# Gated attention and spectral mixing on one core: key differences, the half-scanned pair and output weights handled at other places in the program

## The chip, the core and the metric

The kernel runs on one core of a Trainium2 chip. The metric is the device time of one execution in microseconds (us). A core has five engines with instruction streams of their own: TensorE (PE, with its weight loads as PEld), VectorE (DVE), ScalarE (ACT), GpSimd (POOL) and SyncE (SP), which here only issues DMAs. Each stream runs in order, and an instruction that waits holds up everything behind it in that stream.

## The reference, cut to what matters

```python
x = A_x                                              # (1, 2048, 512)
g = sigmoid((x * gate_w).sum(-1, keepdims=True))
qkv = x @ wqkv                                       # 32 heads of 16
a = softmax(q @ k.T / 4) @ v                         # full attention per head
a = a.reshape(1, 2048, 512) @ wo
b = cr @ (x @ wr.T) - ci @ (x @ wi.T)                # real part of a 2-D Fourier transform
out = g * a + (1 - g) * b                            # cr, ci: 2048 x 2048
```

The weights of the projections are scaled by 64, so scores are large and the softmax needs the maximum of every row.

## The kernel before, in words

All products are done in fp32r with each operand split into a rounded part (hi) and a rest (lo); hi·hi, hi·lo and lo·hi are added. A product of one 128x512 tile therefore takes 12 steps of two matmuls each (`products`, `halves_of` at L180; the two matmuls of a step use the upper and the lower half of the array). One such step is called a **slot** here, and 12 slots a **unit**. `beside()` is called after each slot. It counts slots, runs whatever `after(n, f)` has put off by n slots, and puts in a **scan** when the pace says so. A scan is a score tile of one head pair (two matmuls, 48 rows each) of which DVE takes the row maxima; there are 64 scans a pair and 16 pairs. `scan_at(3.9)` asks for one scan every 3.9 slots.

The program has these stages in order.

1. **Projections** (0 to about 303 us): first q and k (`project_t`), then v (t = 0 to 15), then x·wr and x·wi (`project_s`, 16 units each). ACT copies a unit's two half sums out of PSUM (tags xy, two buffers), POOL adds them, ACT and POOL split them and SP stores them to DRAM. Scans 0 to about 184 run beside these units.
2. **Spectral products** (to about 711 us): 96 units of `coef` for the first 24 of 32 half tiles. The scans 192 to 691 are **folded**: the keys of two key blocks are replaced by one block and a difference of keys (kf_d), ACT takes a relu of the difference scores and DVE adds and reduces in one instruction (L153, L155). In the middle the operands in SBUF are swapped for the second half (`renew`).
3. **Attention** (to the end): 512 steps, 32 a head pair. A step has the scores of one key block (L637), three ACT exponentials (L641, L645), the product with the values (L652) and, up to step 331, one more plain scan (L130). From step MIX = 333 on the other spectral products and, from OUT = 461 on, the output projection (`mix_heads`) are put between.

Three things matter for the change.

- **Differences of keys.** In `project_t` for k the sum s of an odd block c is followed by `fold_keys` (L346): POOL subtracts the two sums that are kept in `half`, ACT makes hi (L215 eh), POOL or DVE makes lo (fl), SP stores both (L356). There are eight folds, two beside the first four k units and six beside the last twelve; during these twelve the pace is SLOW_PACE = 5.2.
- **The half-scanned pair.** FRONT = 692 scans are done when stage 2 ends, so pair 10 is scanned to 52 of 64 with folded keys and needs plain keys for the last 12. `load_scan(10)` (L860, loads at L95 in SP's queue) does that after the loop, into buffers of tag stk (six buffers, two a pair). `load_scan_beside(11)` has loaded pair 11 on ACT's queue shortly before, and step 2 of the attention loads pair 11 once more.
- **Output weights and sums.** `output_operands` is a generator of which one part runs at each step from OUT - 12 on: load a block of wo (tag craw, two buffers), cast it on DVE in the next step (L697, L713), subtract in the one after (L699, L715). `output_rows` loads rows of the attention output (L724), `load_y` (L737) loads two blocks of 1 MB of spectral sums at OUT - 3.

SP's queue holds almost all DMA issues, and so an issue that waits for a buffer holds up all later ones.

Of the kernel before, what the change touches and what calls it, by code (L numbers as in the profile page):

```python
# [18 lines left out]
P = 128  # L19
S = 2048  # L20
# [18 lines left out]
FOLD_PACE = 2.18  # L39
SLOW_PACE = 5.2  # L40
# [7 lines left out]
def build(tc, x, xT, wqkv, wo, wrT, wiT, cr, ci, gate, out):  # L48
    nc = tc.nc
    with ExitStack() as ctx:  # L50
# [7 lines left out]
        k_d = [dram.tile([P, 2, S], F32, name=f"k_d{f}") for f in range(ND)]  # L58
        kf_d = [dram.tile([P, 2, S], F32, name=f"kf_d{f}") for f in range(ND)]
# [22 lines left out]
        scanned, used = {}, {}  # L82
# [107 lines left out]
        with ExitStack() as pf:  # L190
# [34 lines left out]
            def beside():  # L225
# [89 lines left out]
            with ExitStack() as px:  # L315
# [30 lines left out]
                half = {}  # L346

                def fold_keys(f, c):

                    a, b = half.pop(c - 1), half.pop(c)  # L350
                    hi = ep.tile([P, 512], F32R, tag="eh", name="eh", bufs=3)
                    lo = ep.tile([P, 512], F32R, tag="ty", name="fl")
                    nc.gpsimd.tensor_sub(a, a, b)

                    def store(i, v):
                        nc.sync.dma_start(kf_d[f][:, i, (c - 1) * 512:c * 512], v.bitcast(F32))  # L356

                    after(7, nc.scalar.copy, hi, a)
                    after(12, (nc.vector if f else nc.gpsimd).tensor_sub, lo, a, hi.bitcast(F32))
                    after(13, store, 0, hi)  # L360
                    after(16, store, 1, lo)

                def project_t(w, dst, f, c, ps=None):
# [5 lines left out]
                    s = rp.tile([P, 512], F32, tag="raw", name="s") if folded else ep.tile([P, 512], F32, tag="ty", name="s")  # L369
# [92 lines left out]
                scan_at(PACE)  # L462
# [16 lines left out]
                for t in range(NB):  # L479
                    load_xn(t)  # L480
                    after(30, gate_sum, t)
# [44 lines left out]
            with ExitStack() as py:  # L526
# [22 lines left out]
                for n, (ph, t, u) in enumerate(coef):  # L549
# [6 lines left out]
                    if n == len(coef) - 2 * NU:  # L556
                        load_use(0)
# [14 lines left out]
                    def renew(s):  # L572
                        split_operand(s, early.pop(s), nc.gpsimd if s % 4 == 3 else nc.vector)
# [26 lines left out]
        with ExitStack() as pa:  # L600
# [88 lines left out]

            def output_operands():  # L690

                for f in range(ND - 1):
                    raw = ap.tile([P, D], F32, tag="craw", name="wor", bufs=2)
                    nc.sync.dma_start(raw, wo[f * P:f * P + P, :].rearrange("(h e) m -> e h m", e=DH))
                    yield
                    w = [block(6 + 2 * f + i) for i in range(2)]
                    nc.vector.tensor_copy(w[0], raw)  # L697
                    yield
                    nc.vector.tensor_sub(w[1], raw, w[0].bitcast(F32))  # L699
                    w2.append(w)  # L700
                for n in range(3):
                    raw = ap.tile([P, D], F32, tag="craw", name="wor", bufs=2)
                    base = D - (8, 4, 2)[n] * DH
                    if n:
                        nc.vector.memset(raw, 0.0)
                        for c, j, r in quads:
                            nc.sync.dma_start(raw[r:r + DH, :], wo[base + DH * j:base + DH * j + DH, :])
                    else:
                        for r in (0, 64):
                            nc.sync.dma_start(raw[r:r + 64, :], wo[base:base + 64, :].rearrange("(h e) m -> e h m", e=DH))  # L710
                    yield
                    w = [block(12 + 2 * n + i) for i in range(2)]
                    nc.vector.tensor_copy(w[0], raw)  # L713
                    yield
                    nc.vector.tensor_sub(w[1], raw, w[0].bitcast(F32))  # L715
                    w4.append(w)
# [142 lines left out]
            if FRONT % SCANS:  # L859
                load_scan(FRONT // SCANS)  # L860
# [21 lines left out]
            for step in range(NP * PERIODS):  # L882
# [115 lines left out]
```

## Time and profile before

| | |
|---|---|
| median of three runs | 1801.66 us (1800.71 to 1802.69) |
| the profiled execution, its own time | 1800.78 us |
| its span in the trace | 1799.0 us |
| PE busy | 1731.1 us, 96% |
| ACT, DVE, POOL busy | 1453.3, 1165.8, 708.6 us |
| mean granted clock of PE | 0.985 |

The profile is of one execution. Busy time of PE is from the modelled ends of matmuls, so that a PE which is "busy" may still wait a little; the number of matmuls in a stretch of given length tells more. "Idle before" names what ended an idle time. A row of the timeline gives the start in us, the length, the engine, the line and what was done. The granted clock is 1.00 at full speed and 0.50 where PE was held to half.

### The profile page before, as it was taken

To read this page: it belongs to the slowest core of one execution; us is meant where nothing else is said; L and a number is where in the kernel's file an instruction comes from. 1 tells how busy PE (TensorE), PEld (TensorE's weight loads), DVE (VectorE), ACT (ScalarE), POOL (GpSimd) and SP (SyncE) were. 2 spreads that over 40 slices of the span, in tenths; PEclk is the share of its full clock that TensorE was granted. 3 is DMA by queue.
4 is the path that set the end of the run, shared out by engine and by line. 5 is a ranking of instruction groups with operands and counts; after the bars stand their busy time and mean duration, and the time that the engine had idled before them with its cause. 6 is when DMAs were issued, how large, how long until landed. Compare 5 with 4: busy or idle time off the path is not lost.

```text
span 1799.0 us, 35571 instructions
## 1 busy us (share of the span) xinstructions
PE 1731.1 (96%) x13640; PEld 1024.8 (57%) x13640; DVE 1165.8 (65%) x1893; ACT 1453.3 (81%) x2386; POOL 708.6 (39%) x808
## 2 busy tenths in 40 slices
PE   8988999999998998799999999999999999997998
PEld 6867877888886897234333333333334555553554
DVE  6689999999998886566666666666663211212234
ACT  6444434888887786799999999999999888885885
POOL 4676637555555564023232323232332322322212
PEclk9999999999999999899999999999999999998999
DMA  8684427333355445441432333515313344265422
GB/s 285 219 285 114 127 92 234 110 116 107 106 156 147 131 137 121 76 72 39 82 63 56 63 58 58 98 20 98 75 34 74 91 89 97 62 145 154 115 51 97
DMA packets 124250, 195.87 MB, mean 109 GB/s; under 512 B 53824, under 2 KB 56368, under 8 KB 116976
## 3 DMA queue, kind: packets, MB, share of 16 engines
q1 hardware_dynamic: 81488, 155.78, 32.7%
q0 software_dynamic: 38496, 19.47, 5.1%
q10 hardware_dynamic: 4096, 18.36, 3.9%
q8 instruction: 107, 1.75, 0.5%
q14 instruction: 63, 0.52, 0.1%
HBM read 131.47 MB, written 61.61 MB: 107 GB/s over the span
## 4 chain that ended last, share of the span: by engine, by line
PE 61%; DMA 3%; issue 2%; DVE 2%; POOL 1%; ACT 0%; SPq 0%; DVEq 0%; POOLq 0%; ACTq 0%
PE pvb L652 26%; PE s L637 17%; PE s L180 7%; PE s L130 4%; PE xy L180 4%; PE s L149 2%; DMA lc<-ob 1%; DMA wor<-wo 1%; DMA qs<-q_d 0%; DVE mx L132 0%; DVE fold L155 0%; DMA b<-o_d 0%; DVE y L742 0%; SPq L95 0%; POOL lc L660 0%
## 5 line engine op out<-in xcount | busy, mean ns | idle before, releaser
L132 DVE TENSOR_REDUCE mx<-s 128x2 f32<-128x1024 f32 x517 | 620.3, 1223 | 225.0 <-PE s L130 224.7
L641 ACT ACTIVATE eb<-s 128x1024 f32<-128x1024 f32 x512 | 578.7, 1130 | 85.5 <-PE s L637 85.5
L645 ACT ACTIVATE e<-s 128x512 f32<-128x512 f32 x1024 | 609.4, 707 | 1.5 <-PE s L637 1.5
L652 PE MATMUL pvb<-e,va 128*17 128x512 f32 x2048 | 518.6, 600 | 0.0
L652 PE MATMUL pvb<-eb,va 128*17 128x512 f32 x2048 | 518.5, 600 | 0.0
L637 PE MATMUL s<-qs,ks 50*128 50x512 f32 x2048 | 428.4, 438 | 1.6 <-DVE ty L592 1.6
L637 PEld LDWEIGHTS s<-qs,ks 50*128 50x128 f32 x2048 | 213.5, 185 | 371.4 <-ACT eb L641 279.2
L155 DVE CUSTOM_DVE_ANT_0 fold<-s,fold 128x512 f32<-128x512 f32 x500 | 336.8, 690 | 34.9 <-PE s L149 17.3
L153 ACT ACTIVATE fold<-s 128x512 f32<-128x512 f32 x500 | 294.4, 602 | 77.3 <-PE s L149 53.4
L130 PE MATMUL s<-ks,qs 48*128 48x512 f32 x1034 | 217.4, 400 | 30.0 <-DMA qs<-q_d 14.2
L149 PE MATMUL s<-ks,qs 48*128 48x512 f32 x1000 | 237.6, 406 | 6.6 <-DVE mx L155 6.4
L660 POOL DMA_DIRECT2D lc<-ob x124 | 63.1, 515 | 337.1 <-DVE ob L657 337.0
L652 PEld LDWEIGHTS pvb<-eb,va 128*17 128x17 f32 x2048 | 69.2, 96 | 190.7 <-issue 182.3
L149 PEld LDWEIGHTS s<-ks,qs 48*128 48x128 f32 x1000 | 128.9, 184 | 48.1 <-DVE mx L155 22.1
L667 POOL DMA_DIRECT2D r_d<-lc x31 | 18.1, 585 | 297.5 <-DVE lc L666 297.5
L130 PEld LDWEIGHTS s<-ks,qs 48*128 48x128 f32 x1034 | 104.1, 185 | 45.8 <-DVE mx L132 20.1
L180 PE MATMUL xy<-w,b 64*128 64x512 f32 x768 | 108.0, 398 | 0.6 <-ACT ty L401 0.6
L400 ACT ACTIVATE tx<-xy 128x512 f32<-128x512 f32 x48 | 28.7, 598 | 94.4 <-PE xy L180 83.3
L742 DVE SCALAR_TENSOR_TENSOR y<-s,g,y 128x512 f32<-128x512 f32 x50 | 36.6, 748 | 83.0 <-PE s L180 82.4
L180 PE MATMUL s<-b,chi 64*128 64x512 f32 x542 | 85.3, 390 | 0.3 <-ACT chi L952 0.3
L180 PEld LDWEIGHTS xy<-w,b 64*128 64x128 f32 x768 | 75.4, 190 | 16.8 <-ACT ty L401 1.5
L669 POOL DMA_DIRECT2D rb<-r_d x124 | 60.5, 495 | 61.3 <-DMA r_d<-lc 61.2
(754 smaller groups left out, 2375.2 us busy)
## 6 DMA issues: line engine op xcount, KB each, us to landing
craw<-ci SPq DMA_DIRECT2D x64, 256.0 KB
craw<-cr SPq DMA_DIRECT2D x60, 256.0 KB
ks<-k_d SPq DMA_DIRECT2D x46, 256.0 KB
qs<-q_d SPq DMA_DIRECT2D x46, 256.0 KB
ab_d<-ab SPq DMA_DIRECT2D x32, 256.0 KB
y_d<-y SPq DMA_DIRECT2D x32, 256.0 KB
o_d<-oh POOLq DMA_DIRECT2D x28, 256.0 KB, 9.5
o_d<-ol POOLq DMA_DIRECT2D x28, 256.0 KB, 14.2
```

What stands on the lines that cost most here:

```text
L130: nc.tensor.matmul(ps[:, j, :], qs[b:b + 48, qb * P:(qb + 1) * P], ks[b:b + 48, c * 512:(c + 1) * 512], start=True, stop=True)
L132: nc.vector.tensor_reduce(mx[p][:, :, qb, c], ps, axis=AX.X, op=ALU.max)
L149: nc.tensor.matmul(ps, qs[b:b + 48, qb * P:(qb + 1) * P], ks[b:b + 48, c * 512:(c + 1) * 512], start=True, stop=True)
L153: nc.scalar.activation(fold[j], ps, AF.Relu)
L155: nc.vector.tensor_tensor_reduce(out=fold[j], in0=ps, in1=fold[j], scale=1.0, scalar=-3.0e38, op0=ALU.add, op1=ALU.max, accum_out=mx[p][:, ...
L180: nc.tensor.matmul(ps[j], lhs[r], rhs[r], start=first, stop=last)
L637: nc.tensor.matmul(pss[j], ks[b:b + 50, kb * P:(kb + 1) * P], qs[b:b + 50, q0:q0 + 512], start=True, stop=True)
L641: nc.scalar.activation(e, ps, AF.Exp, scale=SCALE)
L645: nc.scalar.activation(e[j], pss[j], AF.Exp, scale=SCALE)
L652: nc.tensor.matmul(pvb[r:r + VC, :], va[:, kb, 2 * p + j, :], es[c][j], start=kb == 0, stop=kb == NB - 1, tile_position=(0, r))
L660: nc.gpsimd.dma_start(lc[32 * n:32 * n + 32, :], ob[r + DH:r + VC, :].rearrange("p (s e) -> p s e", e=16))
L669: nc.gpsimd.dma_start(rb[r:r + DH, :], r_d[p][h][n:n + 1, :].to_broadcast([DH, 512]))
```

## The change

- `fold_keys` no longer runs beside the k units. Each sum s of k is stored to a new DRAM tensor ks_d (one DMA a unit). In the x·wr units with odd t, 6 slots into the unit, `fold_keys` loads two blocks of ks_d back (SP), 12 slots later POOL subtracts, 5 later ACT casts hi, 1 later POOL makes lo, in place in the second block; hi and lo are stored 1 and 5 slots later. The next fold starts 1 slot after that and uses the same two buffers (tag el).
- s of k takes a buffer of tag ty (two) in place of raw (three); the v weights are split on POOL in place of DVE; SLOW_PACE is gone, so the pace stays 3.9 through the k units. FOLD_PACE goes from 2.18 to 2.23, and scan 192 waits for stage 2.
- Pair 11 is not loaded ahead any more. Pair 10's plain keys are loaded eight units before stage 2 ends, ahead of `load_use(0)`.
- `renew` issues the cast, and the subtraction 4 slots later.
- The six blocks of wo are loaded in two groups of three, at OUT - 10 and OUT + 4, and cast from two steps later on; the second `output_rows` goes from OUT - 4 to OUT + 1, the first `load_y` from OUT - 3 to OUT - 25.

```diff
-FOLD_PACE = 2.18
-SLOW_PACE = 5.2
+FOLD_PACE = 2.23
...
+                if seen[0] == FOLDED[0] and not beds:
+                    pace[1] = 0.0
...
-                    if n % SCANS == 36:
+                    if n % SCANS == 36 and n - n % SCANS + SCANS < FRONT:
                         load_scan_beside(n // SCANS + 1)
...
-                def fold_keys(f, c):
-
-                    a, b = half.pop(c - 1), half.pop(c)
-                    hi = ep.tile([P, 512], F32R, tag="eh", name="eh", bufs=3)
-                    lo = ep.tile([P, 512], F32R, tag="ty", name="fl")
-                    nc.gpsimd.tensor_sub(a, a, b)
+                def fold_keys(f, g):
+
+                    a, b = (ep.tile([P, 512], F32, tag="el", name="fa") for _ in range(2))
+                    c = 2 * g
+                    for i, v in enumerate((a, b)):
+                        nc.sync.dma_start(v, ks_d[f][:, (c + i) * 512:(c + i + 1) * 512])
+                    hi = ep.tile([P, 512], F32R, tag="gb", name="fh", bufs=1)
+                    lo = b.bitcast(F32R)
...
-                    after(7, nc.scalar.copy, hi, a)
-                    after(12, (nc.vector if f else nc.gpsimd).tensor_sub, lo, a, hi.bitcast(F32))
-                    after(13, store, 0, hi)
-                    after(16, store, 1, lo)
+                    after(12, nc.gpsimd.tensor_sub, a, a, b)
+                    after(17, nc.scalar.copy, hi, a)
+                    after(18, nc.gpsimd.tensor_sub, lo, a, hi.bitcast(F32))
+                    after(19, store, 0, hi)
+                    after(23, store, 1, lo)
...
-                    s = rp.tile([P, 512], F32, tag="raw", name="s") if folded else ep.tile([P, 512], F32, tag="ty", name="s")
+                    s = ep.tile([P, 512], F32, tag="ty", name="s")
...
                     if folded:
-                        half[c] = s
-                        if c % 2:
-                            after(6, fold_keys, f, c)
+                        after(10, nc.sync.dma_start, ks_d[f][:, c * 512:(c + 1) * 512], s)
...
-                    if n == 0:
-                        scan_at(SLOW_PACE)
                     if n == 3:
-                        load_w(wv, wqkv[:, 1024:1536], 48, nc.vector)
+                        load_w(wv, wqkv[:, 1024:1536], 48, nc.gpsimd)
...
+                    if t % 2:
+                        after(6, fold_keys, *divmod(t // 2, 2))
                     project_s(wr, t, 1.0, to_rhs(0))
...
                     if n == len(coef) - 2 * NU:
+                        unfolded[FRONT // SCANS], loads = row_loads(FRONT // SCANS, nc.sync)
+                        for load in loads:
+                            load()
                         load_use(0)
...
-                        split_operand(s, early.pop(s), nc.gpsimd if s % 4 == 3 else nc.vector)
+                        raw = early.pop(s)
+                        ah[s], al[s] = block(2 * s), block(2 * s + 1)
+                        nc.scalar.copy(ah[s], raw)
+                        after(4, (nc.gpsimd if s % 4 == 3 else nc.vector).tensor_sub, al[s], raw, ah[s].bitcast(F32))
...
-            if FRONT % SCANS:
-                load_scan(FRONT // SCANS)
+            scanned.update(unfolded)
...
-                if step >= OUT - 12:
+                if OUT - 10 <= step < OUT - 4 or step >= OUT + 4:
                     next(operands, None)
-                if step in (OUT - 12, OUT - 4):
-                    output_rows((step - OUT + 12) // 8)
-                if step in (OUT - 3, (NP - 1) * PERIODS):
+                if step in (OUT - 12, OUT + 1):
+                    output_rows(int(step > OUT))
+                if step in (OUT - 25, (NP - 1) * PERIODS):
```

How instructions stand now, at three places. The first is SP's queue at the end of stage 2. k_d_77 and q_d_73 hold pairs 8 to 11, k_d_75 and q_d_71 pairs 0 to 3 (so these rows load pair 0 for use), yre and y belong to the last spectral tiles. Before:

```order
L113 DMA qs<-m_d_83 1x64x32 x2
L563 DMA yre<-y_d_132 128x512
L215 DMA y_d_132<-y 128x512
L563 DMA yre<-y_d_132 128x512
L215 DMA y_d_132<-y 128x512 x2
L95 DMA ks<-k_d_77 32x1x2048
L95 DMA qs<-q_d_73 32x2048
L95 DMA ks<-k_d_77 16x2048
L95 DMA qs<-q_d_73 16x2048
```

And now:

```order
L95 DMA ks<-k_d_77 32x1x2048
L95 DMA qs<-q_d_73 32x2048
L95 DMA ks<-k_d_77 16x2048
L95 DMA qs<-q_d_73 16x2048
L95 DMA ks<-k_d_75 32x1x2048
L95 DMA qs<-q_d_71 32x2048
L95 DMA ks<-k_d_75 16x2048
L95 DMA qs<-q_d_71 16x2048
```

The loads of pair 10 stood behind the store of the last spectral sum; now they stand ahead of pair 0's, behind the last load of coefficients and ahead of the yre and y rows. (Four loads are for one head of a pair. The second piece has those of pair 10's second head and pair 0's first.)

The second place is POOL's stream in the x·wr units; ab is the sum of a unit, w the split of wi, fa and fh belong to a fold. Before:

```order
L500 TENSOR_TENSOR ab<-tx,ty 128x512 x5
L280 TENSOR_TENSOR w_2550<-wraw,w_2549 128x512
L500 TENSOR_TENSOR ab<-tx,ty 128x512
L280 TENSOR_TENSOR w_2550<-wraw,w_2549 128x512
L500 TENSOR_TENSOR ab<-tx,ty 128x512
```

And now, from the third fold on:

```order
L498 TENSOR_TENSOR ab<-tx,ty 128x512 x2
L215 TENSOR_TENSOR fa<-fa 128x512
L282 TENSOR_TENSOR w_2550<-wraw,w_2549 128x512
L215 TENSOR_TENSOR fa<-fa,fh 128x512
L498 TENSOR_TENSOR ab<-tx,ty 128x512
L282 TENSOR_TENSOR w_2550<-wraw,w_2549 128x512
L498 TENSOR_TENSOR ab<-tx,ty 128x512
L215 TENSOR_TENSOR fa<-fa 128x512
L282 TENSOR_TENSOR w_2550<-wraw,w_2549 128x512
L215 TENSOR_TENSOR fa<-fa,fh 128x512
```

Every second unit has two more POOL instructions, and twice the split of a weight block stands between the two.

The third is DVE's stream where the output weights are prepared; L781 (now L791) takes in the sums of the last spectral tile, L742 (now L752) those of the first output tile. Before:

```order
L715 TENSOR_TENSOR b_20740<-wor,b_20739 128x512
L705 MEMSET wor 128x512
L713 CAST b_20793<-wor 128x512
L781 SCALAR_TENSOR_TENSOR y<-s_20399,gm,y 128x512 x2
L715 TENSOR_TENSOR b_20794<-wor,b_20793 128x512
L742 SCALAR_TENSOR_TENSOR y_20742<-s_20834,g,y_20742 128x512 x2
```

And now:

```order
L722 CAST b_20575<-wor 128x512
L723 TENSOR_TENSOR b_20576<-wor,b_20575 128x512
L791 SCALAR_TENSOR_TENSOR y<-s_20423,gm,y 128x512 x2
L752 SCALAR_TENSOR_TENSOR y_20197<-s_20815,g,y_20197 128x512 x2
L663 COPY ob<-pvb 128x512
L709 MEMSET wor 128x512 x2
L752 SCALAR_TENSOR_TENSOR y_20197<-s_20932,g,y_20197 128x512 x2
L722 CAST b_20901<-wor 128x512
```

The cast of the last block no longer stands ahead of L781; the second three blocks are cast behind the first output tiles.

More of the change, by code (lines that the diff above doesn't have):

```diff
@@ L58, in build @@
         k_d = [dram.tile([P, 2, S], F32, name=f"k_d{f}") for f in range(ND)]
+        ks_d = [dram.tile([P, S], F32, name=f"ks_d{f}") for f in range(ND)]
         kf_d = [dram.tile([P, 2, S], F32, name=f"kf_d{f}") for f in range(ND)]
@@ L79, in build @@
         nc.vector.memset(ones, 1.0)
-        scanned, used = {}, {}
+        scanned, used, unfolded = {}, {}, {}
         def row_loads(p, queue, keys=k_d):
@@ L344, in split_x @@
                     split(*xs[d, c], raws[d][:, c * 512:(c + 1) * 512], nc.vector)
-                half = {}
-                def fold_keys(f, c):
-                    a, b = half.pop(c - 1), half.pop(c)
-                    hi = ep.tile([P, 512], F32R, tag="eh", name="eh", bufs=3)
-                    lo = ep.tile([P, 512], F32R, tag="ty", name="fl")
-                    nc.gpsimd.tensor_sub(a, a, b)
-                    def store(i, v):
-                        nc.sync.dma_start(kf_d[f][:, i, (c - 1) * 512:c * 512], v.bitcast(F32))
-                    after(7, nc.scalar.copy, hi, a)
-                    after(12, (nc.vector if f else nc.gpsimd).tensor_sub, lo, a, hi.bitcast(F32))
-                    after(13, store, 0, hi)
-                    after(16, store, 1, lo)
+                def fold_keys(f, g):
[5 more added lines that the diff above has]
+                    lo = b.bitcast(F32R)
+                    def store(i, v):
+                        nc.sync.dma_start(kf_d[f][:, i, c * 512:(c + 1) * 512], v.bitcast(F32))
+                    after(12, nc.gpsimd.tensor_sub, a, a, b)
[3 more added lines that the diff above has]
+                    after(23, store, 1, lo)
                 def project_t(w, dst, f, c, ps=None):
@@ L480, in build @@
                     load_xn(t)
-                    after(30, gate_sum, t)
+                    after(30 if t < NB - 1 else 18, gate_sum, t)
                     if t == 2:
@@ L688, in build @@
             direct, w4 = {}, []
+            raws_ = []
             def output_operands():
[L692 to L707, printed above, removed]
-                    else:
[L709 to L716, printed above, removed]
+                for n in range(2 * ND - 2):
+                    b = [block(6 + 2 * n + i) for i in range(2)]
+                    raw = (ap.tile([P, D], F32, tag="craw", name="wor", bufs=2) if n == ND - 2 else
+                           ap.tile([P, D], F32, tag="take", name="wor", bufs=3))
+                    if n < ND - 1:
+                        nc.sync.dma_start(raw, wo[n * P:n * P + P, :].rearrange("(h e) m -> e h m", e=DH))
+                    else:
+                        base = D - (8, 4, 2)[n - ND + 1] * DH
+                        if n >= ND:
+                            nc.vector.memset(raw, 0.0)
+                            for c, j, r in quads:
+                                nc.sync.dma_start(raw[r:r + DH, :], wo[base + DH * j:base + DH * j + DH, :])
+                        else:
+                            for r in (0, 64):
+                                nc.sync.dma_start(raw[r:r + 64, :],
+                                                  wo[base:base + 64, :].rearrange("(h e) m -> e h m", e=DH))
+                    raws_.append((raw, b))
+                    if n % (ND - 1) == ND - 2:
+                        yield
+                        yield
+                        for raw, b in raws_:
+                            yield
+                            nc.vector.tensor_copy(b[0], raw)
+                            nc.vector.tensor_sub(b[1], raw, b[0].bitcast(F32))
+                            (w2 if n < ND - 1 else w4).append(b)
+                        raws_.clear()
+                        yield
```

1 line of the change is left out of this document (removed).

## The prediction, made before the changed kernel was run

> **What bounds the kernel now.** I read the busy time first, then stretches of the span, then what waits in the stretches that fall short, and at those places the timeline.
>
> ```profile
> PE 1731.1 (96%) x13640; PEld 1024.8 (57%) x13640; DVE 1165.8 (65%) x1893; ACT 1453.3 (81%) x2386; POOL 708.6 (39%) x808
> ```
>
> PE is the bound almost throughout, and the change removes no matmul: 692 scans still stand before the attention. So the time can only change by PE's idle time, and by stretches in which its clock is halved. The stretches show where these are (columns: length, busy time and instructions of PE, PEld, DVE, ACT, POOL, granted clock, DMA share, GB/s):
>
> ```profile
> 90.00:135.00 45.00, 38.34 (x302) 30.59 (x300) 38.04 (x36) 20.41 (x38) 35.12 (x26) 0.96 0.84 285
> 135.00:180.00 45.00, 39.69 (x317) 31.81 (x316) 43.01 (x37) 20.46 (x47) 30.16 (x24) 0.92 0.42 114
> 180.00:225.00 45.00, 45.00 (x388) 37.34 (x386) 44.93 (x44) 19.10 (x43) 27.99 (x22) 1.00 0.43 127
> 495.00:540.00 45.00, 44.61 (x378) 38.04 (x376) 41.61 (x124) 37.30 (x65) 23.56 (x24) 1.00 0.50 154
> 540.00:585.00 45.00, 40.41 (x315) 30.22 (x311) 40.42 (x107) 35.94 (x66) 26.45 (x24) 1.00 0.53 149
> 720.00:765.00 45.00, 36.34 (x244) 12.87 (x246) 23.26 (x23) 32.32 (x51) 1.14 (x2) 0.83 0.47 74
> 765.00:810.00 45.00, 45.00 (x338) 16.80 (x334) 30.33 (x27) 45.00 (x72) 12.14 (x21) 1.00 0.41 71
> ```
>
> An undisturbed 45 us of projections holds 388 matmuls. From 90 to 180 us there are 619, worth 71.8 us: **18.2 us are lost** there. The swap (540 to 585) lost (378 - 315) x 45/378 = 7.5 us against its neighbour. Steps of the attention are 1.875 us (72 ACT instructions, three a step, in 45 us).
>
> **Half-scanned pair.** The end of the loop, from the timeline:
>
> ```profile
> 712.62 0.94 PE L637 MATMUL s<-qs,ks 50*128 50x512 f32 x4 [1.62 <-DVE ty L592]
> 715.70 0.57 SPq L95 DMA_DIRECT2D ks<-k_d  x1
> 723.50 0.76 PE L130 MATMUL s<-ks,qs 48*128 48x512 f32 x1 [9.95 <-DMA qs<-q_d]
> 728.53 0.76 PE L130 MATMUL s<-ks,qs 48*128 48x512 f32 x1 [4.27 <-DMA qs<-q_d]
> 729.76 1.02 ACT L641 ACTIVATE eb<-s 128x1024 f32<-128x1024 f32 x1 [14.34 <-PE s L637]
> 738.67 1.04 ACT L641 ACTIVATE eb<-s 128x1024 f32<-128x1024 f32 x1
> ```
>
> Pair 10's loads start at 715.70 and the first scan of the attention ends its wait at 728.53. With the loads issued eight units earlier (at least 8 x 12 slots of two matmuls, 192 of the 378 that the stretch 495 to 540 holds in 45 us, so over 22 us; the buffers are those of pair 8, whose scans are long over), the scan can follow the scores of 712.62, at about 713.6: 15.0 us. Then three steps took 738.67 - 729.76 = 8.9 us where 3 x 1.875 = 5.6 is usual, because the clock was halved: 3.3 us more. PE's idle time before 712.62 (1.62 us) and the start of the exponentials stay. I take **-17**, between -15 (half clock stays) and -18.3. What is late next is the first exponential, which stays on its own pace. [...] Pair 10's 8 issues and pair 0's 14 stand ahead of the last yre and y_d rows on SP, which have 8 units to spare; costed at nothing, 4 us if not.
>
> **Output weights.**
>
> ```profile
> 1632.06 1.08 ACT L645 ACTIVATE e<-s 128x512 f32<-128x512 f32 x2
> 1636.43 1.08 ACT L645 ACTIVATE e<-s 128x512 f32<-128x512 f32 x2
> ```
>
> ```profile
> 1641.87 0.61 PE L652 MATMUL pvb<-eb,va 128*17 128x512 f32 x2
> ...
> 1657.59 2.07 PE L180 MATMUL s<-b,b 64*128 64x512 f32 x8 [13.15 <-DVE y L781]
> ...
> 1666.48 0.61 PE L652 MATMUL pvb<-eb,va 128*17 128x512 f32 x2
> ```
>
> ```profile
> 1655.66 0.43 DVE L713 CAST b<-wor 128x512 fp32r<-128x512 f32 x1 [14.13 <-DMA wor<-wo]
> ```
>
> By the same exponentials two steps on (the first pair of rows), two steps with spectral work take 4.37 us. PE waits for L781, which stands on DVE behind a cast that waits for a block of wo; that block's loads were issued behind two 1 MB loads of sums. At 4.37 us a pair of steps the value product of 1666.48 would start at 1641.87 + 2 x 4.37 = 1650.6: 15.9 us, the half clock behind the gap included. In the change the sums go first, and three blocks are loaded at once with three steps (6.5 us) before the first cast; in front of L781 no cast waits. A load of a block issued behind the first output rows may still be late by a few us, and the second group's ten issues have 6.5 us too. I take **-15**, between -11 (a 4 us wait at the second group) and -15.9.
>
> **k and v units (90 to 180 us).**
>
> ```profile
> PEld s L130 <- DVE mx L132: 7.8, 5, 2.5
> PE s L130 <- DVE mx L132: 5.9, 4, 2.1
> ACT eh L215 <- DMA kf_d<-eh: 4.1, 1, 4.1
> ```
>
> ```profile
> 156.93 5.18 DVE L172 CAST chi<-mt 128x32 fp32r<-128x32 f32 x1
> ```
>
> ```profile
> 160.80 1.26 POOL L472 TENSOR_TENSOR xg<-xn,gb 128x512 f32<-128x512 f32 x1
> 168.76 1.29 POOL L476 TENSOR_TENSOR va<-tx,ty 128x512 f32<-128x512 f32 x1 [6.69 <-ACT ty L401]
> ```
>
> Three losses can be told. (1) DVE's subtractions for folds and weights wait for ACT, and scans behind them hold PE: these instructions leave DVE, so most of about 6 us goes. (2) DVE's cast of pair 0's maxima, 0.2 us of work, took 5.18 us and ended when POOL, busy without a gap, went idle at 162.06; with the halved clock after it, about 7 us. At a pace of 3.9 in place of 5.2 scan 63 comes earlier, ahead of the splits of wr that filled POOL, so I expect the cast to be held for two POOL instructions at most: 5 us go. (3) Stores are slow here (DMA share 0.84): ACT waits 4.1 us. The change adds as many stores (16 of ks_d for 16 of the folds), and s now has two buffers where it had three, while eh is used two thirds as often; I let this loss stay. **-10.5**, between -3 (only the scans' waits shrink by half) and -15.
>
> **Folds in the x·wr units.** New work: 8 folds x (2 loads, POOL, ACT, POOL, 2 stores), hidden only if a fold keeps up with its two units, 2 x 3.46 = 6.9 us by the row of 13 units in 45 us:
>
> ```profile
> L400 ACT ACTIVATE tx<-xy 128x512 f32<-128x512 f32 x13 | 7.8, 599 | 25.4 <-PE xy L180 25.4
> ```
>
> The second buffer holds lo until it is stored, and the next fold's second load waits for that store. So there is a closed chain: store, load, POOL 1.29, ACT 0.62, POOL 1.29 and some 0.4 between. For the two DMAs of 256 KB the trace gives bounds:
>
> ```profile
> rb<-r_d POOLq DMA_DIRECT2D x124, 32.0 KB, 2.0
> r_d<-lc POOLq DMA_DIRECT2D x31, 8.0 KB, 1.7
> ```
>
> ```profile
> 53.95 0.32 SPq L380 DMA_DIRECT2D q_d<-el  x1
> 86.31 0.45 SPq L356 DMA_DIRECT2D kf_d<-eh  x1
> ```
>
> ```profile
> 56.93 1.29 POOL L215 TENSOR_TENSOR el<-s,eh 128x512 fp32r<-128x512 f32 x1 [0.85 <-DMA q_d<-el]
> 93.32 0.62 ACT L215 CAST eh<-s 128x512 fp32r<-128x512 f32 x1 [4.12 <-DMA kf_d<-eh]
> ```
>
> Small DMAs take 1.7 and 2.0 us; a 256 KB store took 2.9 us (53.95 to the wait's end at 56.9) in a full stretch and 6.9 (86.31 to 93.2) beside a 1 MB load. Here the share is 0.43, so I take 2.2 for the store and 2.5 for the load: 2.2 + 2.5 + 3.6 = 8.3 us, 1.4 more than 6.9. Seven times that is 9.8. Twice the split of a wi block (ACT 0.62, POOL 1.29) stands between a fold's POOL instructions: +3.8. The second fold meets pair 2's loads and the 1 MB of wi: +2. POOL and ACT wait in order, so ACT's copies of xy come late and PE waits once the second xy buffer is used up, which forgives about 2.1 us (a unit less the two copies). **+13**, between +2 and, at 6.9 us for either DMA everywhere, +75.
>
> **The rest.** In `renew` DVE no longer waits for ACT, but its subtractions and POOL's remain: **-2** of 7.5 (0 to -6). New order of stores before 60 us, s in two buffers: **+0.5** (-1 to +4). Shift of plain scans, pace 2.23, dropped load of pair 11: same scans, 0.
>
> **The sum.** -17 - 15 - 10.5 + 13 - 2 + 0.5 = -31 from the profiled execution's 1800.78, which is 0.88 below the median of the runs; from the median **1771 us** (1801.66 - 31 = 1770.7).
>
> **The rivals.**
> (a) The folds are hidden: the chain is 7 us or less, the fold term +2. For it: light DMA traffic. Against: the in-place second buffer. 1760 us.
> (b) DVE's cast of pair 1's maxima is held as at 156.93. It now falls on the x·wr units with the wi splits, where POOL has 14 instructions of 1.29 us in some 16 us; 7 us more, 1778. For it: the 5.18 us row. Against: a POOL that waits for a fold's loads leaves gaps. [...]
> (c) Waits stay at the three old places (half clock at 713, blocks of wo late by 4 us, k units gain 4 only): -15 - 11 - 4 + 13 - 1.5 = -18.5, 1783.
> (d) **Slower:** the fold chain runs at the store times of the full stretch all the way, as the folds themselves fill the queues (8.4 MB more in 56 us, 150 GB/s on 127). At 5.5 us for either DMA the chain is 14.6, 7 x 7.7 + 5.8 - 2.1 = 57.6 in place of 13: -44 + 57.6, 1815. It turns slower than before at about 12.8 us a chain (44 = 7 x 5.8 + 3.7). Against: as the chain slows, so does its traffic.
> (e) Pair 10's loads still hold the first scan, because they wait for a buffer: the first term is 0, 1788.
>
> **How the numbers follow.** My forecast 0.56, (a) 0.13, (b) 0.10, (c) 0.11, (d) 0.07, (e) 0.03. The forecast's own range is 1763 to 1780. The range for 8 in 10 takes in (a) and (c) with the unknown prices around them: 1754 to 1790. About 0.2% (3.6 us) is what a measurement of this kernel can tell from no change. Slower by more: the most of (d), 0.06. Within: 0.01, the milder end of (d). Faster: the rest, 0.93.
>
> **What would show it.** Right: no wait for qs or wor of over 2 us at the two places, clock 1.00 there; 90 to 180 us with over 660 matmuls; in the x·wr units ACT waiting for POOL fa and POOL for DMA fa about 1 us at each fold, and units 3.5 us long elsewhere. Wrong: x·wr units at 3.5 us throughout (a), a cast of 5 us at the second shift (b), or units of over 6 us (d).

## The result, and the profile after

The changed kernel takes **1772.84 us** (median of four runs, 1771.38 to 1774.15) where the kernel before takes 1801.18 (1800.01 to 1802.69). The ratio is 0.9842, with a 95% interval of 0.9825 to 0.9859, so it is faster by 1.6%. The forecast was 1771. The profiled executions differ by 28.1 us, 1800.78 against 1772.70, where the sum said 31.

The first view is again that of stretches, this time with bounds at the same points of both programs: ACT's copies of the last q unit, of the last k, v, x·wr and x·wi unit, of the 12th and the 16th half tile of the spectral products (the swap lies between these two), then the exponentials of steps 0, 32, 460 and 464. Columns as in the prediction. Before, the last twelve k units, v, x·wr, x·wi, the swap, the start of the attention and the four steps at the output weights:

```profile
74.71:122.81 48.10, 43.52 (x351) 35.43 (x349) 41.44 (x38) 24.32 (x45) 39.02 (x29) 0.96 0.73 256
122.81:189.47 66.66, 59.27 (x481) 48.06 (x480) 62.95 (x55) 28.91 (x65) 46.51 (x37) 0.95 0.51 140
189.47:246.08 56.61, 56.61 (x486) 45.61 (x484) 56.51 (x57) 21.47 (x44) 28.33 (x23) 1.00 0.36 114
246.08:302.89 56.81, 56.01 (x482) 44.78 (x480) 56.28 (x51) 25.09 (x46) 34.34 (x27) 1.00 0.64 194
...
504.30:576.68 72.38, 68.72 (x558) 54.40 (x556) 66.58 (x186) 58.59 (x106) 39.27 (x38) 1.00 0.48 146
711.09:791.68 80.59, 63.96 (x445) 23.63 (x446) 41.82 (x40) 61.69 (x97) 12.49 (x17) 0.87 0.42 69
1641.76:1666.36 24.60, 11.45 (x68) 4.77 (x66) 2.91 (x5) 7.89 (x13) 2.03 (x3) 0.65 0.82 219
```

The same of the changed kernel:

```profile
73.46:120.43 46.97, 45.06 (x379) 36.90 (x377) 44.63 (x39) 21.81 (x40) 35.29 (x28) 1.00 0.84 282
120.43:175.94 55.51, 55.23 (x470) 43.68 (x470) 55.20 (x53) 28.29 (x64) 45.31 (x36) 1.00 0.47 152
175.94:255.19 79.25, 63.81 (x496) 48.70 (x494) 61.07 (x58) 24.98 (x50) 45.71 (x37) 0.94 0.57 172
255.19:314.00 58.81, 56.14 (x468) 46.59 (x466) 54.95 (x49) 25.29 (x47) 36.99 (x29) 0.97 0.69 208
...
513.33:581.43 68.10, 66.82 (x553) 57.21 (x551) 62.71 (x182) 57.29 (x104) 39.05 (x40) 1.00 0.47 148
715.81:780.28 64.47, 62.12 (x445) 23.24 (x446) 41.80 (x40) 61.47 (x97) 12.48 (x17) 0.97 0.36 62
1629.51:1638.26 8.75, 8.75 (x68) 3.98 (x66) 1.74 (x3) 7.80 (x14) 0.00 (x0) 1.00 0.60 154
```

The gain stands in three places and a large part of it is given back in one. Length after less length before, in us: k units -1.1; v units -11.2; **x·wr units +22.6**; x·wi units +2.0; swap -4.3; start of the attention **-16.1**; output weights **-15.9**. That is -24.0; the spans differ by 1799.0 - 1770.9 = 28.1, and the other 4.1 lie outside these stages: 1.3 before the first of them, which begins at 73.46 in place of 74.71, 2.1 in the spectral products ahead of the swap, and the rest in the attention.

Scans were also moved between stages, so a second number is of use: what a stage lost, its length less its matmuls at 45/388 us each. The k units went from 48.10 - 351 x 0.116 = 7.4 to 3.0, the v units from 10.9 to 1.0, the x·wr units from 0.2 to 21.7.

In the x·wr units these waits stand, for PE, ACT and POOL (us in total, times, longest):

```profile
PE xy L180 <- ACT ty L402: 16.1, 9, 3.7
```

```profile
ACT fh L215 <- POOL fa L215: 43.8, 8, 8.5
```

```profile
POOL fa L215 <- DMA fa<-ks_d: 20.5, 7, 5.8
```

And the first of POOL's two instructions of the eight folds, with the first and the last start:

```profile
L215 POOL TENSOR_TENSOR fa<-fa x8: 1261/1275/1294, 187.6 to 260.4; 128x512 f32<-128x512 f32 x8
```

Seven folds took 260.4 - 187.6 = 72.8 us, 10.4 each, where two units take 6.9. The order of the waits is as forecast: POOL waits for a load, ACT's cast of hi waits for POOL, ACT's copies stand behind that cast, PE waits for a copy. The loads behind the first fold, then one whole turn, in SP's queue and on POOL:

```profile
191.28 6.15 SPq L353 DMA_DIRECT2D fa<-ks_d  x2
...
214.43 0.32 SPq L358 DMA_DIRECT2D kf_d<-fa  x1
214.80 1.97 SPq L353 DMA_DIRECT2D fa<-ks_d  x2
...
225.11 0.32 SPq L358 DMA_DIRECT2D kf_d<-fa  x1
```

```profile
220.05 1.27 POOL L215 TENSOR_TENSOR fa<-fa 128x512 f32<-128x512 f32 x1 [1.90 <-DMA fa<-ks_d]
222.57 1.27 POOL L282 TENSOR_TENSOR w<-wraw,w 128x512 fp32r<-128x512 f32 x1 [1.25 <-ACT w L281]
223.79 1.30 POOL L215 TENSOR_TENSOR fa<-fa,fh 128x512 fp32r<-128x512 f32 x1
```

The rest of a fold is stored at 214.43. The two loads of the next follow; the second ends its issue at 216.77, 2.3 us on. POOL has them at 220.05, 3.3 us later. Two POOL instructions, ACT's cast and a split of wi between them end with the next store at 225.11, 5.1 us later: 10.7 in all. Behind the first fold the wait for the buffer is longest: the row at 191.28 is two issues, of which the second ends 6.5 us after the store at 190.91.

Over the seven turns, from the store at 190.91 to that at 263.67, the parts add up so: 23.3 us from a store to the end of the next fold's second issue (2.3 to 6.5 each), 22.8 from there to POOL's start (3.0 to 4.1 each), 26.6 from there to the next store (3.3 to 5.1 each).

At the two other places PE waits no longer for a load. DVE still waited 6.1 us for the first blocks of wo, until 1614.69, but that is 15 us ahead of the four steps, and PE is busy throughout these (8.75 of 8.75 us). At the start of the attention PE waits twice, 1.6 and 0.7 us, and a short stretch at half clock stayed:

```profile
720.00:724.00 4.00, 4.00 (x22) 1.19 (x24) 1.68 (x2) 2.88 (x5) 0.45 (x1) 0.57 0.78 201
```

### The profile page after: what moved, and what is told of

It is laid out like the page before. It is cut to its first block, busy times and chain, and to the rows that moved or that the text cites. A ratio compares the mean times of both kernels' runs of the same rounds, so it can differ in the third digit from the quotient of the medians.

```text
span 1770.9 us, 35629 instructions
## 1 busy us (share of the span) xinstructions
PE 1724.9 (97%) x13640; PEld 1032.9 (58%) x13640; DVE 1151.2 (65%) x1876; ACT 1451.5 (82%) x2386; POOL 716.4 (40%) x818
## 4 chain that ended last, share of the span: by engine, by line
PE 86%; DMA 6%; DVE 2%; POOL 2%; issue 2%; ACT 1%; SPq 0%; DVEq 0%; POOLq 0%; ACTq 0%
PE pvb L658 28%; PE xy L180 20%; PE s L643 18%; PE s L180 8%; PE s L149 7%; PE s L130 6%; DMA fa<-ks_d 2%; DMA kf_d<-fa 1%; POOL fa L215 1%; DVE mx L132 1%; DMA raws<-xT 1%; DMA ks_d<-s 1%; DMA raws<-wqkv 0%; DMA q_d<-el 0%; POOL s L215 0%
## 5 line engine op out<-in xcount | busy, mean ns | idle before, releaser
L132 DVE TENSOR_REDUCE mx<-s 128x2 f32<-128x1024 f32 x524 | 628.8, 1223 | 228.9 <-PE s L130 227.7
L149 PEld LDWEIGHTS s<-ks,qs 48*128 48x128 f32 x1000 | 129.0, 184 | 40.9 <-DVE mx L155 16.2
L130 PEld LDWEIGHTS s<-ks,qs 48*128 48x128 f32 x1048 | 107.8, 185 | 15.2 <-DVE mx L132 5.7
L752 DVE SCALAR_TENSOR_TENSOR y<-s,g,y 128x512 f32<-128x512 f32 x50 | 36.6, 748 | 76.4 <-PE s L180 75.8
```

The lines of the kernel that those rows point to most:

```text
L130: nc.tensor.matmul(ps[:, j, :], qs[b:b + 48, qb * P:(qb + 1) * P], ks[b:b + 48, c * 512:(c + 1) * 512], start=True, stop=True)
L132: nc.vector.tensor_reduce(mx[p][:, :, qb, c], ps, axis=AX.X, op=ALU.max)
L149: nc.tensor.matmul(ps, qs[b:b + 48, qb * P:(qb + 1) * P], ks[b:b + 48, c * 512:(c + 1) * 512], start=True, stop=True)
```

## The experiments

Each kernel was timed beside runs of the kernel before on the same chip. One thing ahead of all: the stage lengths in the expectations (80 us for x·wr, 62.7 for v, 11.5 lost in k) were read with bounds four units later than their names say, as the copies of four early units go by another name. Measured lengths below have the right bounds, those of the tables above; where a verdict comes near the difference, in experiment 4, both are given. Each experiment has one profiled execution, so a difference of a stage between two kernels also holds what differs from one execution to the next.

**1. A fold's own buffers.**

```diff
-a, b = (ep.tile([P, 512], F32, tag="el", name="fa") for _ in range(2))
+a, b = (rp.tile([P, 512], F32, tag="raw", name="fa") if g % 2 else ep.tile([P, 512], F32, tag="el", name="fa")
+        for _ in range(2))
```

> The changed kernel, with the folds loading in turn into the two buffers of tag el and into two of the three of tag raw, which are free in the x·wr units; nothing else. Theory (a closed chain: the second load of a fold waits until the rest of the fold before is stored out of the same buffer): the loads are issued at their slot, a fold keeps up with its two units, and the x·wr units, now 80 us for 16 units, come down to 56 to 60; total 1749 to 1754 us. Rival 1 (a load alone, about 3.5 us from issue to the wait's end, is as long as the 12 slots it is given, so ACT still waits at each fold): half of it, 1758 to 1763. Rival 2 (the work that the folds add on POOL and ACT, or their DMA traffic, sets the pace): 1768 to 1774.

1770.45 us, ratio 0.9841 (0.9815 to 0.9867), that of the changed kernel. The x·wr units:

```profile
176.24:253.44 77.20, 65.05 (x496) 50.45 (x494) 61.49 (x58) 24.98 (x51) 45.73 (x37) 0.91 0.57 177
```

2.1 us of 22.6 came back. The theory as I had it, that the shared buffer alone closes the chain, falls: with the buffer free the loads still went out only behind the store. SP's queue in this kernel:

```profile
225.37 0.32 SPq L359 DMA_DIRECT2D kf_d<-fa  x1
225.74 0.93 SPq L354 DMA_DIRECT2D fa<-ks_d  x2
```

The loads stand behind the store of the rest in the same in-order queue, and that store waits for POOL. So they are issued when the fold before is done, buffer or not.

**2. The same with a unit more between loads and fold.**

```diff
-after(12, nc.gpsimd.tensor_sub, a, a, b)
-after(17, nc.scalar.copy, hi, a)
-after(18, nc.gpsimd.tensor_sub, lo, a, hi.bitcast(F32))
-after(19, store, 0, hi)
-after(23, store, 1, lo)
+after(24, nc.gpsimd.tensor_sub, a, a, b)
+after(29, nc.scalar.copy, hi, a)
+after(30, nc.gpsimd.tensor_sub, lo, a, hi.bitcast(F32))
+after(31, store, 0, hi)
+after(35, store, 1, lo)
```

> As fold_two_pairs, and each fold computed 12 slots (one unit) later behind its loads. Theory (closed chain only): as fold_two_pairs within 2 us. Rival 1 (a load is as long as the 12 slots): 5 to 10 us faster than fold_two_pairs, since the loads now have 24 slots; total 1748 to 1753. Rival 2 (added work or traffic): 1768 to 1774, as the changed kernel.

**1757.08 us**, ratio 0.9765 (0.9741 to 0.9789), 13.4 us faster than fold_two_pairs, which was timed beside it. The x·wr units and SP's queue:

```profile
176.94:241.05 64.11, 60.28 (x502) 46.39 (x500) 60.91 (x59) 24.98 (x50) 44.36 (x36) 1.00 0.71 216
```

```profile
214.42 0.91 SPq L354 DMA_DIRECT2D fa<-ks_d  x2
...
221.56 0.32 SPq L359 DMA_DIRECT2D kf_d<-fa  x1
```

The loads of the next fold now go out 7.1 us ahead of the store that they stood behind. Rival 2 (added work or traffic sets the pace) is out: all the work and 216 GB/s are still there, the clock is back at 1.00, and the length is 7.5 us above that of the kernel before in place of 22.6 (what is left may be theirs). The theory of the buffer alone, which expected under 2 us, is out as well. Rival 1 (a load longer than its 12 slots) named the direction, but 5 to 10 us and 1748 to 1753; so nobody's range was met, and this experiment can't tell rival 1 from the order of the queue. The next two tell queue order from slots.

**3 and 4. The folds' stores on POOL's queue**, with one pair of buffers and with two. Slots stay those of the changed kernel.

```diff
-nc.sync.dma_start(kf_d[f][:, i, c * 512:(c + 1) * 512], v.bitcast(F32))
+nc.gpsimd.dma_start(kf_d[f][:, i, c * 512:(c + 1) * 512], v.bitcast(F32))
```

> The changed kernel, with the folds' stores (hi and rest) issued on POOL's DMA queue in place of SP's; the folds keep their one pair of buffers. After fold_two_pairs (80 to 76 us only) and fold_two_pairs_ahead (62 us) the theory is that two links close the chain, and either is enough: a fold's second load needs the buffer of the rest before it, and on SP both loads stand behind that store, which waits for POOL. Theory: the buffer still closes it, the x·wr units stay at 75 to 82 us, total 1767 to 1775. Rival (only SP's order counted): the x·wr units fall to 60 to 65 us, total 1753 to 1758.

1790.47 us, ratio 0.9948 (0.9932 to 0.9965).

> fold_two_pairs with the folds' stores on POOL's DMA queue: both links are open now, and the slots of loads and folds are those of the changed kernel (12 slots from the loads to the subtraction). Theory (two links): the x·wr units come to 61 to 67 us, total 1754 to 1761. Rival (a load needs more than its 12 slots, and only the 24 slots of fold_two_pairs_ahead helped): 72 us or more, total 1765 or more.

1764.64 us, ratio 0.9812 (0.9789 to 0.9834). The x·wr units with one pair:

```profile
176.31:268.62 92.31, 66.46 (x500) 50.55 (x498) 65.09 (x59) 25.00 (x51) 52.70 (x51) 0.91 0.48 145
```

and with two:

```profile
175.20:247.16 71.96, 63.14 (x496) 49.65 (x494) 66.78 (x58) 25.03 (x51) 52.62 (x51) 0.93 0.63 194
```

So, for one and two pairs of buffers: 79.3 and 77.2 us with the stores on SP, 92.3 and 72.0 with them on POOL. Either link alone keeps the chain closed; both must be open. The rival that only SP's order counts would have had 60 to 65 for the first and is out. For the second the times alone don't decide: the theory had 61 to 67 us and 1754 to 1761, the rival that a load needs over 12 slots 72 or more and 1765 or more, and 71.96 us (68.0 by the bounds of the expectation) and 1764.64 lie between the two. POOL's waits decide. No slot changed, and yet POOL waits for the loads only once (or twice, if a wait of 2.4 us that the profile puts down to a load of qs is one too), where in the changed kernel it waited seven times, 20.5 us in all:

```profile
POOL fa L215 <- DMA fa<-ks_d: 2.3, 1, 2.3
```

So 12 slots are enough for nearly all loads as soon as both links are open. Both kernels came out slower than the theory's range. POOL's rows show one reason: a store costs POOL 0.56 us and other instructions stand between lo and its store. Another is that the cast of pair 1's maxima was held in both, for 3.62 us in the first and as follows in the second:

```profile
220.42 5.51 DVE L172 CAST chi<-mt 128x32 fp32r<-128x32 f32 x1
```

```profile
220.36 1.31 POOL L499 TENSOR_TENSOR ab<-tx,ty 128x512 f32<-128x512 f32 x1
...
224.62 1.26 POOL L215 TENSOR_TENSOR fa<-fa 128x512 f32<-128x512 f32 x1
226.61 1.27 POOL L215 TENSOR_TENSOR fa<-fa,fh 128x512 fp32r<-128x512 f32 x1 [0.73 <-ACT fh L215]
```

That is the prediction's rival (b): the cast of pair 1's maxima begins beside a POOL instruction and ends when POOL, busy without a gap, goes idle at 225.88. How much of the 72.0 us each reason is worth was not measured.

**5. The two places of the attention, alone.** The kernel before with pair 10's keys loaded early (as in the change's diff) and

```diff
-if step in (OUT - 3, (NP - 1) * PERIODS):
+if step in (OUT - 25, (NP - 1) * PERIODS):
```

> The kernel before with two parts of the change alone, which lie 900 us apart in the trace: pair 10's plain keys loaded eight units before the end of stage 2 (and pair 11's load there dropped), and the first sums loaded at OUT - 25 in place of OUT - 3; the six blocks of wo stay as before. Theory: the wait for qs at the start of the attention goes (-16 us), and the wait for wor goes whole (-14 to -16), since only the two 1 MB loads of sums stood ahead of that block; total 1768 to 1772. Rival (a block still waits: two buffers, loaded one step before its cast): -16 and only -4 to -10 at the output weights, total 1775 to 1782.

1779.23 us, ratio 0.9894 (0.9865 to 0.9924). The start of the attention and the four steps at the output weights:

```profile
709.08:774.75 65.67, 63.42 (x445) 23.58 (x446) 41.81 (x40) 61.60 (x97) 12.47 (x17) 0.95 0.34 61
1624.26:1641.05 16.79, 10.24 (x68) 4.65 (x66) 2.92 (x5) 7.89 (x13) 2.24 (x3) 0.80 0.84 181
```

80.59 to 65.67 is 14.9 of the 16.1 us that the changed kernel gains there (64.47); experiments 6 and 7, with the same loads, have 65.35 and 64.23. At the output weights only 24.60 - 16.79 = 7.8 of 15.9 us went: the rival. The two 1 MB loads of sums were half of that wait.

**6. Rows and renew too.**

```diff
-if step in (OUT - 12, OUT - 4):
-    output_rows((step - OUT + 12) // 8)
+if step in (OUT - 12, OUT + 1):
+    output_rows(int(step > OUT))
...
-split_operand(s, early.pop(s), nc.gpsimd if s % 4 == 3 else nc.vector)
+raw = early.pop(s)
+ah[s], al[s] = block(2 * s), block(2 * s + 1)
+nc.scalar.copy(ah[s], raw)
+after(4, (nc.gpsimd if s % 4 == 3 else nc.vector).tensor_sub, al[s], raw, ah[s].bitcast(F32))
```

> before_pair10_sums with two more parts of the change: the second rows of the attention output loaded at OUT + 1 in place of OUT - 4 (the blocks of wo still one by one), and renew with the subtraction four slots behind the cast. before_pair10_sums left 8.0 of 15.9 us at the output weights, with the last block's loads issued behind six loads of rows. Theory: those six loads are the rest of the wait; without them it falls to 0 to 2 us there, and the regrouping of the blocks is worth little. Rival (loading one step ahead into two buffers is the rest): 5 to 8 us stay. renew: the swap gains 2 to 5 us by the theory that DVE's waits for ACT's casts cost PE time; 0 by its rival, that the rest of the swap's loss is the work itself. Together some 1763 to 1768 against 1801.

1779.75 us, ratio 0.9881 (0.9857 to 0.9904): no faster than experiment 5, and 12 us above the range expected. The profiled execution, 1772.89, was the fastest; the other three took 1778.88 to 1780.95. The v units, the swap and the output weights:

```profile
125.93:186.36 60.43, 58.20 (x478) 45.38 (x478) 57.91 (x55) 29.32 (x66) 46.92 (x37) 0.97 0.52 155
501.61:572.14 70.53, 68.47 (x557) 54.76 (x555) 66.78 (x186) 58.61 (x105) 38.52 (x39) 1.00 0.46 146
1621.66:1638.26 16.60, 10.22 (x68) 4.63 (x66) 4.05 (x7) 7.90 (x14) 3.36 (x4) 0.79 0.53 140
```

16.60 after 16.79: my theory that the rows were the rest is wrong. DVE's timeline shows what is left:

```profile
1620.62 0.67 DVE L719 CAST b<-wor 128x512 fp32r<-128x512 f32 x1 [3.26 <-DMA wor<-wo]
...
1628.79 0.43 DVE L719 CAST b<-wor 128x512 fp32r<-128x512 f32 x1 [5.95 <-DMA wor<-wo]
1629.13 1.53 DVE L787 SCALAR_TENSOR_TENSOR y<-s,gm,y 128x512 f32<-128x512 f32 x2
```

Each block is loaded after the cast of the one before it, so 5 to 8 us pass between two casts, and L787, which PE waits for, stands behind the last. The swap came from 72.38 to 70.53, 1.8 us against 4.3 in the changed kernel; but experiments 7 and 9, which leave `renew` as it was, have 71.39 and 70.78, so 1.8 is the most that it can be worth here. The v units have the same instructions as in experiment 5, and yet take 60.43 us where they took 66.28 there. DVE's cast of pair 0's maxima took 5.05 us in experiment 5, and here:

```profile
160.40 0.78 DVE L172 CAST chi<-mt 128x32 fp32r<-128x32 f32 x1
```

POOL runs without a gap from 149.85 to 166.12 in this execution, and DVE got in all the same.

**7. The blocks in groups, and the cast of the maxima on ACT.** Experiment 5 with the change's `output_operands` and its steps, the rows left where they were, and

```diff
-lambda: nc.vector.tensor_copy(hi, t),
+lambda: (nc.scalar.copy if p < 3 else nc.vector.tensor_copy)(hi, t),
```

> The kernel before with pair 10's early load and the sums at OUT - 25 (as before_pair10_sums), and two parts more, in other stages. (1) The six blocks of wo in two groups of three, as in the change, with the second rows left at OUT - 4. Theory (a block cannot be cast sooner than a load behind the cast before it, so one block at a time is what was left): the steps OUT - 1 to OUT + 3, 16.8 us in before_pair10_sums and 8.8 in the changed kernel, come to 8.8 to 9.5. Rival (rows and blocks together are needed): 12 or more. (2) The cast of the maxima of pairs 0 to 2 made by ACT in place of DVE. Theory (the 5 us cast is DVE held off by a POOL without gaps, and it costs the v units its length and a stretch at half clock): the v units, 62.7 us, come to 55 to 57. Rival (the next DVE instruction of the kind is held in its place): 61 to 63. Total 1757 to 1765 with both, against 1800.

1767.04 us, ratio 0.9803 (0.9772 to 0.9835), 2 us above the range for both parts together. The v units and the output weights:

```profile
122.48:190.18 67.70, 60.84 (x480) 47.93 (x478) 61.16 (x54) 28.94 (x67) 46.84 (x37) 0.92 0.47 138
1624.45:1633.20 8.75, 8.75 (x68) 3.98 (x66) 1.74 (x3) 7.79 (x13) 2.88 (x3) 1.00 0.37 89
```

8.75, the length in the changed kernel: the groups are the other 8 us, and the move of the rows is worth nothing. The second part failed, as its rival said. DVE in the v units:

```profile
159.43 3.97 DVE L173 TENSOR_TENSOR clo<-mt,chi 128x32 fp32r<-128x32 f32 x1
```

With the cast on ACT it is the subtraction of the same 128x32 tile that takes 3.97 us.

**8. The old pace in the changed kernel.**

```diff
-FOLD_PACE = 2.23
+FOLD_PACE = 2.21
+SLOW_PACE = 5.2
...
+if n == 0:
+    scan_at(SLOW_PACE)
...
+scan_at(PACE)
```

> The changed kernel with the old pace of 5.2 slots a scan from the thirteenth-last k unit on, back to 3.9 behind them (and 2.21 in place of 2.23 in the folded part, so that all 692 scans still fit). Theory (the k and v units gained because the folds and the split of the v weights left DVE): total within 3 us of the changed kernel, 1770 to 1776, and no cast of maxima over 2 us. Rival (the pace did it, by moving the shift of scan 63 away from the splits of wr on POOL): a cast of about 5 us is back between 145 and 165 us, total 1777 to 1781.

1787.08 us, ratio 0.9931 (0.9908 to 0.9954). The cast is back, as the rival had it, and the v units with it:

```profile
123.92:189.22 65.30, 56.76 (x470) 45.80 (x470) 62.57 (x53) 28.63 (x64) 45.13 (x36) 0.95 0.48 142
```

```profile
155.62 7.19 DVE L173 CAST chi<-mt 128x32 fp32r<-128x32 f32 x1
```

65.30 - 55.51 = 9.8 us with the same 470 matmuls, and PE waited 6.7 us in one piece for the maxima behind that cast. The total is 6 us above the rival's range; the profiled execution was the slowest of its kernel (1793.1; the others 1782.5 to 1787.7), so I leave that remainder open.

**9. The new pace in the kernel before.** SLOW_PACE = 3.9, and no folded scan ahead of stage 2.

> The kernel before with the pace of scans kept at 3.9 through the k units (and no folded scan ahead of stage 2, as in the change); folds and v weights stay beside the k units. Theory (the folds' instructions on DVE, ACT and in the queues were the loss there, and more scans only add to DVE's): the k units keep 9 us or more of their loss of 11.5; the cast of pair 0's maxima comes before the splits of wr and takes under 2 us, so the v units lose 2 to 4 us in place of 7.7. Total 1792 to 1799. Rival (the pace alone was the gain): the k units' loss falls to 4 to 5 us, total 1786 to 1791.

1796.79 us, ratio 0.9982 (0.9966 to 0.9998). The k and v units:

```profile
77.15:127.07 49.92, 44.47 (x365) 34.00 (x361) 49.92 (x46) 24.90 (x46) 38.07 (x30) 1.00 0.77 267
127.07:185.42 58.35, 57.45 (x486) 44.89 (x484) 58.31 (x56) 28.57 (x64) 46.32 (x37) 1.00 0.44 144
```

The v units lose 58.35 - 486 x 0.116 = 2.0 us in place of 10.9. The k units lose 7.6. With the old pace, folds and v weights they lost 5.3 to 7.4 in four kernels (7.4 in the kernel before), and with all three changed 3.0 to 4.6 in six (3.0 in the changed kernel): the pace alone does nothing for them. The moved folds and v weights alone do little either, since experiment 8, which has them at the old pace, loses 47.81 - 361 x 0.116 = 5.9. Both together are needed, by these profiles. In this kernel the gain was mostly used up elsewhere (the k units begin 2.4 us later, and stage 2 is longer).

**10. The v weights on DVE again** (`load_w(wv, ..., nc.vector)`).

> The changed kernel with the rests of the v weights made on DVE again, as before. Theory (DVE's instructions that wait for ACT hold the maxima, and scans behind them PE): four such waits come back, 1 to 4 us slower in the k units, 1773 to 1777. Rival (it was the folds and the pace alone): within 1 us.

1776.47 us, ratio 0.9873 (0.9853 to 0.9893). The k units:

```profile
74.12:121.35 47.23, 44.55 (x365) 37.70 (x361) 44.93 (x41) 22.24 (x41) 31.97 (x25) 0.96 0.82 281
```

They lose 4.9 us where the changed kernel loses 3.0, but five other kernels with the k units of the changed kernel lose 3.2 to 4.6, so these profiles do not show a price for this part. The total, 3.6 us more, is in the theory's range, but its interval overlaps that of the changed kernel: it stays open.

**11. Experiment 2 with the cast on ACT.**

> fold_two_pairs_ahead (1757 us) with the cast of the maxima of pairs 0 to 2 made by ACT. Its own casts took 0.6 us and less, so theory and rival alike expect 1753 to 1759; it would be worth 3 to 6 us only in executions where a cast is held as the 5.5 us one of fold_two_pairs_stores_pool was, so the spread of its times should be smaller, under 4 us.

1756.48 us (1751.79 to 1757.17), ratio 0.9741 (0.9714 to 0.9768): no difference from experiment 2 that these runs can tell, and a spread of 5.4 us where under 4 was expected. Its profiled execution, the fastest, kept the full clock at the start of the attention:

```profile
696.48:759.47 62.99, 60.65 (x445) 22.34 (x446) 41.82 (x40) 61.38 (x98) 12.50 (x17) 1.00 0.36 64
```

62.99 against 64.47 us: so the short stretch at half clock is worth about 1.5 us there, by this one pair of executions.

## Why the prediction was right, and where it was not

**Half-scanned pair: -17, measured -16.1.** Experiments 5 to 7 give -14.9, -15.2 and -16.4 for this part. The half clock that the term allowed for stayed, at about 1.5 us where 3.3 went before, so the -18.3 of a full clock was not reached.

**Output weights: -15, measured -15.9.** The size was right, the reason given only half of it. The prediction named the two 1 MB loads of sums; they are 7.8 us (experiment 5). Blocks loaded one by one are the other 8.0 (experiment 7), the second rows nothing (experiment 6).

**k and v units: -10.5, measured -12.3** in length, with 17 more matmuls of scans done in them, so -14.3 of loss (4.4 and 9.9). The cast was short, as forecast, in the changed kernel:

```profile
139.62 0.62 DVE L172 CAST chi<-mt 128x32 fp32r<-128x32 f32 x1
...
140.17 1.29 POOL L282 TENSOR_TENSOR clo__1765<-wraw,chi__1761 128x512 fp32r<-128x512 f32 x1
```

The reason given for it was not the right one. It was to come ahead of the splits of wr that fill POOL; but POOL, with a split of wr among its instructions (the second row), runs without a gap from 137.66 to 145.21 here, and the cast got in when one of POOL's instructions ended at 140.20. The pace has to do with it: at the old pace this cast of pair 0's maxima, or the subtraction behind it, took 4.0 to 7.2 us in four of five profiles (experiment 6 is the fifth), at the new pace 0.39 to 0.77 us in eight of eight. How the pace does it was not shown. The price of 5 us was, if anything, too low: the same v units differ by 5.9 us between experiments 5 and 6, and experiments 8 and 9, which change the pace as well, show 9 to 10. The 4.4 of the k units can't be shared out between the pace and the moved instructions (experiments 8 to 10).

Where POOL was busy without a gap, two small DVE instructions were held in some of the executions: the cast (3.62, 5.05, 5.18, 5.51, 7.19 us), or with the cast on ACT the subtraction behind it (3.97). The maxima, read from PSUM, kept their 1.2 us beside the same POOL work (1.22 and 1.19 us at 154.57 and 155.83 in the kernel before, where POOL had no gap from 145.85 to 162.06). The hold went on over four further POOL instructions of 1.3 us in the kernel before (157.10 to 162.06) and over five in experiment 8 (156.62 to 162.77). What lets DVE in at the end of one POOL instruction in some executions and not in others stays open.

**Folds: +13, measured +24.6** (22.6 and 2.0). This is the step that failed. The path was the one named, and so was the closed chain; its duration was too short. The prediction gave the seven turns 7 x 8.3 + 3.8 + 2 = 63.9 us and forgave 2.1; they took 72.8, and nothing was forgiven (72.8 - 7 x 6.9 = 24.5, all of the loss). Two terms of the chain were too small. The loads, 2.5 us each, 17.5 in all, took 22.8. The wait behind a store, 2.2 us and 2 more at the second fold, 17.4 in all, took 23.3, most of the excess beside pair 2's loads and wi (6.5) and at one later turn (4.3). The compute was the other way, 26.6 where 7 x 3.6 + 3.8 = 29.0 were taken. It also named one link, the buffer, where there are two: the order of SP's queue closes the chain as well, which is why freeing the buffer alone gave 2 us. With both open and loads sent a unit ahead, x·wr takes 7.5 us more than before (64.11 against 56.61) in place of 22.6, and 1.9 of the 7.5 are for 16 more matmuls. The granted clock was also lower in the changed kernel (0.94 in these units; 0.50 from 203.38 to 208 us, behind a wait of PE of 3.71 us), but where a closed chain sets the pace, slower matmuls may mostly fill its waits; how much they add wasn't measured.

**The rest: -1.5, measured -8.4.** The swap gave 4.3 and what lies outside the stages 4.1. Renew alone gave 1.8 at most (experiment 6). The pace of 2.23 and the scans done before stage 2 may be the others; that wasn't tried.

**The rivals.** (a), hidden folds, was wrong for the change and nearly came true in experiment 2. (b) did not happen in the changed kernel (the cast of pair 1's maxima took 0.70 us) but did in experiments 3 and 4. (c): PE waited for neither qs nor wor, though the half clock stayed. (d) had the right direction, at 10.4 us a chain where it turns slower at 12.8. (e) did not happen. That the sum held is in good part luck, because the errors cancel: in length the k and v units came out 1.8 us and the rest 6.9 better than forecast, the folds 11.6 worse.

**The signs.** Between 90 and 180 us there were 741 matmuls, over the 660 named. The clock of 1.00 at the start of the attention did not come (0.57 from 720 to 724), and in the x·wr units the waits were not about 1 us a fold: POOL waited 20.5 us for seven loads and ACT 43.8 us for eight folds.

## What to carry to other kernels

When work is moved to where there seems to be room, write down its loop: what its next load waits for, by buffer and by queue. Here the loads of a fold, which stood behind a store in SP's queue, went out only behind it although their buffers were free (experiment 1: the store at 225.37, the loads at 225.74), so a second buffer gave 2 us of 22.6 until the loads no longer stood behind that store. And open all links of a chain together when testing it: another buffer alone gave 2 us, another queue alone cost 13, both together gave 7, and both links opened on the one queue, with 12 more slots for each load, gave 15.

## What was not expected of the hardware

A DVE instruction that takes 0.18 us as a rule (the cast of maxima, median of 16 in the kernel before) cost the v units 5.9 us (experiments 5 and 6) to 9 or 10 (experiments 8 and 9), by its own 5 to 7 us and the half clock that was measured behind PE's wait for it (0.50 from 163.29 to 166 us in the kernel before, after 4.69 us of waiting). It isn't held every time, with POOL just as busy (0.78 us in experiment 6). When that instruction was taken off DVE, the next one on the same small tile was held for 3.97 us in its place (experiment 7).
